# A spectral block with a feed-forward network: a weight load moved to another queue, and small work dealt out anew to three engines

## The chip, the core and the metric

The kernel runs on one core of a Trainium2 chip. TensorE (PE) multiplies matrices; VectorE (DVE), ScalarE (ACT) and GpSimd (POOL) do the element-wise work; SyncE (SP) issues most DMAs, and ScalarE and GpSimd can issue DMAs from queues of their own. Each engine runs its instructions in the order of the program and waits on semaphores for the others. The metric is the device time of one execution in microseconds; below, "the time" is the median of three runs.

## The reference, cut to what matters

One token block `x` of 2048 x 640 in bf16 goes through two halves, both modulated by a conditioning row `c`:

```
mod = silu(c) @ w_mod                     # 6 rows of 640: sa, ca, ga, sb, cb, gb
h = layernorm(x) * (1 + ca) + sa
x = x + ga * irfft2(rfft2(h) * W)         # W: 2048 x 321, complex
h = layernorm(x) * (1 + cb) + sb
x = x + gb * ((silu(h @ w_gate) * (h @ w_up)) @ w_down)    # 640 -> 1728 -> 640
```

The change touches the last four rows of `mod`: the shift `sb`, the scale `cb` and the gate `gb` of the second half (and it leaves `ga` where it was).

## The kernel before, in words

The 2048 tokens lie as 16 tiles of 128. The order of the work is written out by hand; nothing is reordered by a planner, so each engine's program is the order of the calls in the source.

**First half, to about 36 us.** Statistics and a transform over the 640 columns, then over the 128 rows of each tile; the result is `A_sb` in region `rA`.

**Spectral stage, about 36 to 63 us.** It runs over 21 groups of up to four frequencies. For each group: TensorE's `stage_a` (L567, four products, plus L580 in the last groups), VectorE's two multiplications by the filter (L592), TensorE's `stage_b` (L599), ScalarE's copy out of PSUM (`Y2`, L602), and one or two groups later TensorE's `stage_c` (L620) and a copy `evac` (mostly ScalarE, L637). GpSimd adds a constant to the transposed data before its first use (`sa_add`, L559) and makes copies of rotated values (`rot`, L648). The data of the groups 5 to 20 come from four DMA transposes on SyncE's queue (`t2_dma`, L519), one for four groups each. `stage_b` of group g and of group g + 2 use the same PSUM bank, and `stage_c` of the units (0, 1) and (2, 3) use the same two banks.

The weights of `mod` for this half and the next lie in `wm_r`, four blocks of 640 columns (gate of the first half, then shift, scale and gate of the second). Block 0 comes early. Blocks 1 and 2 (1600 KB, one DMA, L527) and block 3 (L528) stand on SyncE's queue behind the four transposes, and ahead of the tables `Htab` and `RI` (L529, L530) and the weights of the next half (L734 to L746). Blocks 1 and 2 are first read by L580 in group 17 (the fourth last), where `mod_col` computes shift and scale as columns; they end up in `modcols[:, 2]` and `one_p_cb`. Block 3 gives the gate column `modcols[:, 3]` at the end of the stage.

**Tile loop, about 63 to 82 us.** For each tile t: the inverse over rows (L669, L678) for tile t + 2, ScalarE's copy `VT` (L673), the inverse over columns (L1184, L1187), and VectorE's sum with `x` that also gives the row sums (L1189). The PSUM banks of L1184 alternate with t, so tile t + 2 needs the sum of tile t. Between them stand the preparations of the feed-forward network:

- `gdiag`: five diagonal matrices with the gate column (L1196, GpSimd, after tile 0). L1175 multiplies them by ones in tiles 5 and 7, which spreads the gate over all partitions (`gb_bc`), and `wd_fold` (L827) folds it into the down weights.
- The second layernorm of tiles 0 and 1: squares on ScalarE (L761), variance on VectorE (L765 to L767), the power -0.5 on GpSimd (L771), the normalized rows on VectorE (L775), a DMA transpose on SyncE (L789) into `h2T_first`.
- `ln2_mod(0)`: shift and scale of that first chunk, in five pieces of 128 features each. Four run on GpSimd (L797, called after tile 10), the fifth on ScalarE (L803, called after tile 13). L1001 (`gu13`, called in tile 15) is their first reader, one piece for each of its five products.
- `GS[0]`: a sum of two blocks of the gate weights, made by two DMAs from GpSimd's queue (L823), the second adding to the first; called after tiles 8 and 11. L818 reads it in the first chunk.

**Feed-forward network, 82 us to the end.** Four chunks of 2, 4, 4 and 6 tiles, the first with plain products (L1013, L891), the others with a Strassen-like scheme (L1043, L914).

Of the kernel before, what the change touches and what calls it, by code (L numbers as in the profile page):

```python
# [21 lines left out]
NC5 = 5  # L22
# [127 lines left out]
def _rev(ap, free_off, dims):  # L150
    a = ap[:]
    return bass.AP(tensor=a.tensor, offset=a.offset + free_off, ap=[list(a.ap[0])] + [list(d) for d in dims])
# [3 lines left out]
def adaln_block_kernel(ctx, tc, A_x, A_w_r, A_w_i, B_x, B_w_gate, B_w_up, B_w_down, c, w_mod, out):  # L156
    nc = tc.nc
# [26 lines left out]
    modcols = const.tile([P, 4, NC5], F32, name="modcols")  # L184
# [8 lines left out]
    identb = const.tile([P, 128], BF16, name="identb")  # L193
# [19 lines left out]
    wm_r = rM.cut(12800, [NC5, 4, D])  # L213
# [19 lines left out]
    def banks(b, n, shape=None, dt=F32):  # L233
        ap = psum[:, b:b + n, :].rearrange("p b e -> p (b e)")
        if dt == BF16:
            ap = ap.bitcast(BF16)
        if shape is not None:
            ap = ap[:, 0:int(np.prod(shape))]
            if len(shape) > 1:
                ap = ap.rearrange("p (a b) -> p a b", a=shape[0])  # L240
        return ap
# [36 lines left out]
    wm_m = wm_v[:, :, 2 * D:6 * D].rearrange("p k (i d) -> p k i d", i=4)  # L278
# [233 lines left out]
    if True:  # L512
        B2of = {}

        def t2_dma(bi):
            l0 = (1, 16, 32, 64)[bi]
            n = 15 if bi == 0 else 16
            B2b = rL.cut(4096 * bi, [16, 128]) if bi < 3 else rM.cut(6144, [16, 128])
            nc.sync.dma_start_transpose(B2b[:, :n, :], A_sb[:, l0:l0 + n, :, :, :].rearrange("p l t c r -> p l (t c r)"))  # L519
            for i in range(n):  # L520
                B2of[l0 + i] = (B2b, i, l0, n)
# [2 lines left out]
        t2_dma(1)  # L524
        t2_dma(2)
        t2_dma(3)
        nc.sync.dma_start(wm_r[:, :, 1:3, :], wm_m[:, :, 1:3, :])  # L527
        nc.sync.dma_start(wm_r[:, :, 3, :], wm_m[:, :, 3, :])  # L528
        nc.sync.dma_start(Htab[:], H_dram)  # L529
        nc.sync.dma_start(RI[:], RI_dram)  # L530
# [63 lines left out]
        def stage_b(g, PP):  # L594
            n = len(groups[g])
            yps = banks((g + 1) % 2, 1, [4, 128])
            for ps in (1, 0):
                for i in range(n):
                    nc.tensor.matmul(yps[:, i, :], lhsT=_rev(PP, 64 * n * ps + i, [[n, 128]]), rhs=identb[:],  # L599
                                     start=(ps == 1 and i == 0), stop=(ps == 0 and i == n - 1))  # L600
            Y2 = rY.cut(1024 * (g % 4), [4, 128])
            nc.scalar.copy(Y2[:, 0:n, :], yps[:, 0:n, :])  # L602
            return Y2
# [90 lines left out]
        for g in range(NG + 1):  # L694
            if g > 1:
                sa_add(g + 4)
            for W, lo, hi in {0: ((Wv, 80, 81), (Wv, 0, 16)), 1: ((Wv, 16, 32),), 3: ((Wv, 32, 48),), 11: ((Wn, 64, 80),), 13: ((Wv, 64, 80),)}.get(g, ()):
                wsum(W, lo, hi, nc.gpsimd)
                if g == 0 and hi == 81:
                    sa_add(5)  # L700
            if 0 < g < NG - 2:
                PPs[g + 2] = stage_a(g + 2)
            if g == NG - 3:
                nc.vector.tensor_copy(modcols[:, 2, :], psum[:, 2, 192:197])
                nc.vector.tensor_scalar_add(one_p_cb[:], psum[:, 4, 192:197], 1.0)
            if rots:
                l0, n, i = rots.pop(0)
                rot(l0, n, slice(0, 64), nc.gpsimd, (i,))
            if g < NG:
                Y2s[g] = stage_b(g, PPs.pop(g))  # L710
            for u, gs in enumerate(units):
                if gs[-1] + (1 if gs[0] >= NG - 2 else 3 if gs[0] == 4 else 2) == g:
                    stage_c(u)
                    evac(u)
            if g == NG - 3:
                rot(40, 8, slice(0, 64), nc.vector)
            if g == NG - 1:
                for c5 in range(NC5):
                    mod_col(psum[:, 3, 192 + c5:193 + c5], wm_r[:, :, 3], c5)
# [11 lines left out]
        gdiag = rL.cut(10496, [NC5, 128])  # L731
# [52 lines left out]
    def h2T_of(ci):  # L784
        return (h2T_next if ci else h2T_first)[:, 0:chunks[ci][1]]
# [7 lines left out]
    def ln2_mod(ci, cs=range(NC5)):  # L793
        h2T = h2T_of(ci)
        for c5 in cs:
            if ci == 0 and c5 < 4:
                nc.gpsimd.tensor_scalar(h2T[:, :, c5, :], h2T[:, :, c5, :], one_p_cb[:, c5:c5 + 1], modcols[:, 2, c5:c5 + 1],  # L797
                                        ALU.mult, ALU.add)
            elif ci and c5 % 2 == 0 or ci > 1:
                nc.vector.tensor_scalar(h2T[:, :, c5, :], h2T[:, :, c5, :], one_p_cb[:, c5:c5 + 1], modcols[:, 2, c5:c5 + 1],  # L800
                                        ALU.mult, ALU.add)
            else:
                nc.scalar.activation(h2T[:, :, c5, :], h2T[:, :, c5, :], ACT.Identity,  # L803
                                     scale=one_p_cb[:, c5:c5 + 1], bias=modcols[:, 2, c5:c5 + 1])
# [3 lines left out]
    GS = [r.cut(off, [2, GC], F16) for r, off in ((rY, 0), (rE, 25088), (rW, 42496), (rE, 31744))]  # L808
# [13 lines left out]
    def gu_dma(o, w, r, n, first):  # L822
        nc.gpsimd.dma_start(o, w[128 * r:128 * r + 128 * n, 0:GC].rearrange("(c5 dp) f -> dp c5 f", dp=P),  # L823
                            accum_op=ALU.bypass if first else ALU.add)
# [339 lines left out]
    if True:  # L1164
        s1em(2, range(0, 2))
        VTs = {0: s1er(0, 4)}
        s1em(2, range(2, 4))
        VTs[1] = s1er(1)
        for t in range(NT):
            if t and t + 2 < NT:  # L1170
                s1em(t + 2)
                if t in (5, 7):
                    g0, g1 = ((0, 3), (3, 5))[t // 7]
                    gps_ = psum[:, s1b(t + 2) + 1, 128:128 + 128 * (g1 - g0)]
                    nc.tensor.matmul(gps_, lhsT=ones[:], rhs=gdiag[:, g0:g1].rearrange("p a b -> p (a b)"), start=True, stop=True)  # L1175
                VTs[t + 2] = s1er(t + 2)
                if t in (5, 7):
                    nc.scalar.copy(gb_bc[:, 128 * g0:128 * g1], gps_)
            VT = VTs.pop(t)
            if t == NT - 1:  # L1180
                fin13 = gu13(0, at_of(0))
            ops = banks(6 * (t % 2), 2, [4, 256])[:, :, 0:160]
            for h in range(2):
                nc.tensor.matmul(ops[:, 2 * h:2 * h + 2], lhsT=VT[:, 4, :], rhs=RI[:, 1, 2 * h:2 * h + 2, :],  # L1184
                                 start=True, stop=False)
                for rr in range(2):
                    nc.tensor.matmul(ops[:, 2 * h + rr], lhsT=VT[:, 2 * h + rr, :], rhs=RI[:, 0, 2 * h + rr, :],  # L1187
                                     start=False, stop=(rr == 1))
            nc.vector.scalar_tensor_tensor(x1[:, t, :].rearrange("p (m r) -> p m r", r=4), ops.rearrange("p r m -> p m r"), 1.0,  # L1189
                                           x_sb[:, t, :].rearrange("p (m r) -> p m r", r=4), ALU.mult, ALU.add,  # L1190
                                           accum_out=st2[:, t, 0:1])
            if t == 0:
                VTs[2] = s1er(2)
                nc.gpsimd.tensor_copy(warm[:], st2[:, 0, 0:1])
                for c5 in range(NC5):
                    nc.gpsimd.tensor_scalar_mul(gdiag[:, c5], identb[:], modcols[:, 3, c5:c5 + 1])  # L1196
            if t in (8, 11):
                gu_dma(GS[0][:], B_w_gate, t // 11 * 2, 2, t == 8)
            if 1 <= t <= 2:
                ln2_sq(t - 1)  # L1200
            if t == 2:
                ln2_var(0, 2)
                ln2_pow(0, 2)
            if 3 <= t <= 4:
                ln2_xn(0, t - 3)
            if t == 4:
                ln2_tr(0)
                load_gu(512, 1024, (1,))
                load_gu(1024, 1664)
            if t in (5,7,9,11):  # L1210
                ln2_sq(2 + (5,7,9,11).index(t))
            if t in (10, 13):
                ln2_mod(0, range(4) if t == 10 else range(4, 5))
            if t == 14:
                ln2_var(2, 4)
                ln2_pow(2, 4)
            if t in (8, 9, 11, 13, 15):
                wd_fold((t - 7) // 2)
        for o, n, r, w in ((GS[2], 2, 0, B_w_gate), (UG.unsqueeze(1), 1, 4, B_w_gate), (GS[2], 2, 0, B_w_up), (UG.unsqueeze(1), 1, 4, B_w_up)):
            gu_dma(o[:], w, r, n, w is B_w_gate)  # L1220
# [101 lines left out]
```

## Time and profile before

| what | value |
|---|---|
| runs | 248.64, 248.44, 250.56 us; median 248.64 |
| profiled execution | 249.31 us; its span 247.5 us |
| granted TensorE clock | 1.0 throughout |

| stretch (us) | PE busy | DVE busy | ACT busy | POOL busy | GB/s |
|---|---|---|---|---|---|
| 0 to 36 | 34.53 | 27.69 | 23.52 | 26.57 | 332 |
| 36 to 63 (spectral stage) | 25.97 | 23.81 | 22.62 | 17.37 | 277 |
| 63 to 82 (tile loop) | 18.98 | 16.94 | 16.97 | 8.26 | 320 |
| 82 to 105 (first chunk) | 23.00 | 20.26 | 17.45 | 6.08 | 216 |
| 105 to 145 | 40.00 | 37.28 | 28.33 | 6.78 | 29 |
| 145 to 185 | 40.00 | 33.28 | 24.71 | 5.46 | 43 |
| 185 to 247.5 | 59.07 | 48.46 | 34.17 | 7.62 | 22 |

How to read it: a profile is one execution, and its times count from the start of its span. In a timeline row the first two columns are start and length in us, then engine (a "q" marks a DMA issue in that engine's queue), line, operation and operands; what stands in brackets is the idle time of the engine just before it and what ended it. The length of a DMA row is that of its issue, not of the transfer. An engine's next instruction can begin a little before the row of the one ahead ends.

### The profile page before, as it was taken

Reading aid. Unit: us, or ns where it says so; the run is one execution under the profiler, and the core shown is the slowest. Engines: PE = TensorE matmul, PEld = TensorE weight load, DVE = VectorE, ACT = ScalarE, POOL = GpSimd, SP = SyncE. Lnnn points to the kernel's source line nnn. Section 1 sums busy time; section 2 is a strip of 40 time slices with the busy share of each in tenths; the row PEclk is TensorE's granted clock in tenths of the full one; section 3 lists DMA queues with packets and bytes.
Section 4 is the critical chain, followed back from the end, with each engine's and each line's share of the span. In section 5 each row is a group of like instructions: output and inputs, shape, how many; then the busy total and the mean of one; then the engine's idle time right before and its main releaser. Section 6 shows DMA issues by size and latency. Waiting matters only on the chain.

```text
span 247.5 us, 6173 instructions
## 1 busy us (share of the span) xinstructions
PE 241.5 (98%) x2327; PEld 189.7 (77%) x2327; DVE 207.7 (84%) x516; ACT 167.8 (68%) x327; POOL 78.1 (32%) x128
## 2 busy tenths in 40 slices
PE   8999999999999999999999999999999999999994
PEld 3778877989999888688887778887765666656773
DVE  3799699988898998789989977788998787789864
ACT  3778757996989698489774488866246777773220
POOL 8577765993243605002004400000432000004400
PEclk9999999999999999999999999999999999999999
DMA  7999999999999999600005110200411000000111
GB/s 220 396 361 315 307 391 177 179 337 392 295 348 317 298 280 187 139 15 3 0 3 106 53 55 3 57 0 19 93 49 53 3 0 1 4 0 0 53 56 53
DMA packets 45760, 34.74 MB, mean 140 GB/s; under 512 B 21732, under 2 KB 42659, under 8 KB 45347
## 3 DMA queue, kind: packets, MB, share of 16 engines
q1 hardware_dynamic: 43936, 30.00, 42.7%
q0 software_dynamic: 1504, 4.28, 7.4%
q8 instruction: 18, 0.29, 0.5%
q10 hardware_dynamic: 290, 0.08, 0.1%
q14 instruction: 12, 0.09, 0.1%
HBM read 27.05 MB, written 4.72 MB: 128 GB/s over the span
## 4 chain that ended last, share of the span: by engine, by line
PE 89%; DVE 4%; DMA 3%; issue 1%; ACT 0%; POOL 0%; DVEq 0%; SPq 0%; ACTq 0%; POOLq 0%
PE psum L1043 36%; PE psum L914 19%; PE psum L1013 6%; PE psum L891 3%; DMA rM<-in_w_mod_dram 3%; PE psum L669 3%; PE psum L599 2%; PE psum L296 2%; PE psum L1184 2%; PE psum L1187 2%; PE psum L1001 2%; PE psum L567 2%; DVE rE L382 2%; PE psum L318 1%; PE psum L315 1%; PE psum L393 1%
## 5 line engine op out<-in xcount | busy, mean ns | idle before, releaser
L1043 PEld LDWEIGHTS <-rW 128*128 128x128 bf16 (+1 forms) x429 | 42.0, 98 | 12.6
L1043 PE MATMUL psum<-rW 128*128 128x256 bf16 (+1 forms) x247 | 42.2, 287 | 0.0
L940 POOL TENSOR_TENSOR rM<-rM,rL 128x320 f32<-128x320 f32 x6 | 5.4, 906 | 96.6 <-ACT rL L939 96.6
L914 PEld LDWEIGHTS <-rE 128*128 128x128 f16 (+1 forms) x196 | 19.0, 97 | 7.8
L914 PE MATMUL psum<-rE 128*128 128x320 f16 (+1 forms) x147 | 22.9, 299 | 0.0
L592 DVE TENSOR_TENSOR rM<-psum,rW 128x384 bf16<-128x384 f32 (+2 forms) x42 | 20.2, 543 | 2.7 <-PE psum L567 1.2
L1074 ACT COPY rH<-psum 128x384 f32<-128x384 f32 (+2 forms) x27 | 14.0, 517 | 7.4 <-PE psum L1043 6.0
L1081 ACT COPY rX<-psum 128x384 f32<-128x384 f32 (+2 forms) x27 | 14.0, 520 | 7.2 <-PE psum L1043 7.0
L1043 PEld LDWEIGHTS <-rE 128*128 128x128 f16 x156 | 15.3, 98 | 4.7
L1078 DVE TENSOR_TENSOR rH<-psum,rM 128x512 bf16<-128x512 f32 (+1 forms) x24 | 15.0, 624 | 4.4 <-PE psum L1043 2.2
L1097 ACT ACTIVATE rL<-psum 128x384 bf16<-128x384 f32 (+2 forms) x27 | 14.4, 533 | 5.3 <-PE psum L1043 3.4
L1082 DVE TENSOR_TENSOR rX<-psum,rX 128x384 f32<-128x384 f32 (+2 forms) x27 | 16.3, 604 | 1.6 <-ACT rX L1081 1.4
L1068 ACT COPY rM<-psum 128x384 f32<-128x384 f32 (+2 forms) x27 | 13.9, 516 | 4.2 <-PE psum L1043 4.2
L382 DVE SCALAR_TENSOR_TENSOR rE<-rE,mv,psum 128x648 bf16<-128x648 f32 (+1 forms) x17 | 14.2, 840 | 2.1 <-PE psum L318 1.7
L1043 PE MATMUL psum<-rW,rE 128*128 128x256 bf16 (+1 forms) x78 | 15.6, 290 | 0.0
L1043 PE MATMUL psum<-rE,rY 128*128 128x256 f16 (+1 forms) x78 | 15.6, 290 | 0.0
L338 ACT COPY rE<-psum 128x640 bf16<-128x640 bf16 x16 | 11.1, 693 | 6.1 <-PE psum L336 5.1
L1098 ACT ACTIVATE rL<-rX 128x384 bf16<-128x384 f32 (+2 forms) x27 | 15.1, 559 | 0.0
L1013 PE MATMUL psum<-rW 128*128 128x256 bf16 x130 | 14.5, 272 | 0.0
L602 ACT CAST rY<-psum 128x512 bf16<-128x512 f32 (+2 forms) x21 | 11.8, 574 | 3.9 <-PE psum L599 3.6
L1189 DVE SCALAR_TENSOR_TENSOR rM<-psum,rX 128x640 f32<-128x640 f32 x16 | 13.0, 820 | 1.7 <-PE psum L1187 1.6
L883 DVE TENSOR_TENSOR rA<-psum,rM 128x320 bf16<-128x320 f32 (+1 forms) x27 | 12.1, 472 | 2.4 <-PE psum L891 2.3
(223 smaller groups left out, 666.5 us busy)
## 6 DMA issues: line engine op xcount, KB each, us to landing
out_dram<-rA SPq DMA_DIRECT2D x31, 80.0 KB, 1.6
rM<-in_w_mod_dram SPq DMA_DIRECT2D x3, 800.0 KB, 10.2
rX<-in_A_x_dram SPq DMA_DIRECT2D x3, 640.0 KB, 7.4
rA<-in_B_w_down_dram SPq DMA_DIRECT2D x2, 960.0 KB, 14.4
rY<-in_B_w_gate_dram POOLq DMA_DIRECT2D x2, 832.0 KB, 7.9
rM<-in_w_mod_dram SPq DMA_DIRECT2D x1, 1600.0 KB, 7.3
rW<-in_B_w_gate_dram SPq DMA_DIRECT2D x2, 640.0 KB, 7.1
rW<-in_B_w_up_dram SPq DMA_DIRECT2D x2, 640.0 KB, 7.1
```

Of the source, the lines that this page charges most:

```text
L382: nc.vector.scalar_tensor_tensor(Zv[:, h], Cv[:, h], mv[:, t, 0:1], zps[:, h], ALU.mult, ALU.subtract)
L592: nc.vector.tensor_tensor(PP[:, :, hl], xv[:, :, hl], in1, ALU.mult)
L914: nc.tensor.matmul(o, lhsT=lhs[rows(k), k], rhs=rhs[rows(k), k], start=start and k == ks[0], stop=stop and k == ks[-1], skip_group_check=True)
L1013: nc.tensor.matmul(gu[u], lhsT=Wgu[:, u, c5, ff * 128:(ff + 1) * 128], rhs=h2T[:, :, c5, :], start=(c5 == 0), stop=(c5 == NC5 - 1))
L1043: nc.tensor.matmul(o[:, f], lhsT=w, rhs=b, start=(start and f == 0 and i == 0), stop=(stop and f == len(groups[g]) - 1 and i == len(ops) - ...
L1068: nc.scalar.copy(c0, X)
L1074: nc.scalar.copy(c2, X)
L1078: nc.vector.tensor_tensor(c11, Z, c0, ALU.add)
L1081: nc.scalar.copy(c3, X)
L1082: nc.vector.tensor_tensor(c22, Y, c3, ALU.add)
L1097: nc.scalar.activation(g21, X, ACT.Silu, scale=-1.0)
L1098: nc.scalar.activation(g22, c22, ACT.Silu, scale=-1.0)
```

## The change

Four edits:

1. The DMA of blocks 1 and 2 of `wm_r` leaves SyncE's queue and is issued from ScalarE's queue, right behind the `Y2` copy of group 2 of the spectral stage. It waits for no transfer that is still on its way at that point.
2. Of the five pieces of `ln2_mod(0)`, the pieces 0 and 1 stay on GpSimd, piece 2 goes to VectorE (the line L800 of before), pieces 3 and 4 are on ScalarE. The first four are called after tile 12 (before: 10), the fifth after tile 13 as before. In ScalarE's program piece 3 stands between the `VT` copies of tiles 14 and 15, piece 4 behind the latter; in VectorE's, piece 2 stands between the sums of tiles 12 and 13.
3. The five diagonals go from GpSimd to VectorE: two behind the sum of tile 0, three behind that of tile 1.
4. The first DMA of `GS[0]` is called after tile 0 (before: 8), the second after tile 12 (before: 11), there behind the pieces.

No other instruction changes its place in any engine's program.

```diff
@@ spectral stage, SyncE's queue
         t2_dma(3)
-        nc.sync.dma_start(wm_r[:, :, 1:3, :], wm_m[:, :, 1:3, :])
         nc.sync.dma_start(wm_r[:, :, 3, :], wm_m[:, :, 3, :])
@@ loop over the groups
                 Y2s[g] = stage_b(g, PPs.pop(g))
+                if g == 2:
+                    nc.scalar.dma_start(wm_r[:, :, 1:3, :], wm_m[:, :, 1:3, :])
@@ ln2_mod
-            if ci == 0 and c5 < 4:
+            if ci == 0 and c5 < 2:
                 nc.gpsimd.tensor_scalar(...)
-            elif ci and c5 % 2 == 0 or ci > 1:
+            elif ci == 0 and c5 == 2 or ci and c5 % 2 == 0 or ci > 1:
                 nc.vector.tensor_scalar(...)
             else:
                 nc.scalar.activation(...)
@@ tile loop
                 nc.gpsimd.tensor_copy(warm[:], st2[:, 0, 0:1])
-                for c5 in range(NC5):
-                    nc.gpsimd.tensor_scalar_mul(gdiag[:, c5], identb[:], modcols[:, 3, c5:c5 + 1])
-            if t in (8, 11):
-                gu_dma(GS[0][:], B_w_gate, t // 11 * 2, 2, t == 8)
+                gu_dma(GS[0][:], B_w_gate, 0, 2, True)
+            if t < 2:
+                for c5 in range(2 * t, 2 + 3 * t):
+                    nc.vector.tensor_scalar_mul(gdiag[:, c5], identb[:], modcols[:, 3, c5:c5 + 1])
@@ tile loop, later
-            if t in (10, 13):
-                ln2_mod(0, range(4) if t == 10 else range(4, 5))
+            if t in (12, 13):
+                ln2_mod(0, range(4) if t == 12 else range(4, 5))
+            if t == 12:
+                gu_dma(GS[0][:], B_w_gate, 2, 2, False)
```

## The prediction

> **What bounds it now.** The page's first part has TensorE busy 98% of the span, so time is lost only where TensorE stands still or is given more to do. I read the chain that ended last, in order of time, from 47 us on:
>
> ```profile
> 47.29 0.59 ACT rY L602
> 48.06 7.32 DMA rM<-in_w_mod_dram
> 55.43 0.40 PE psum L580 x10
> ```
>
> Columns: start, length, what. From 55.43 the chain stays on TensorE up to 244 us; this is the last place where a transfer holds it. The 7.32 us is the load's whole length; what it costs is in the list of waits (total, times, longest), two rows for one wait:
>
> ```profile
> PEld L580 <- DMA rM<-in_w_mod_dram: 0.8, 1, 0.8
> PE psum L580 <- DMA rM<-in_w_mod_dram: 0.6, 1, 0.6
> ```
>
> TensorE's timeline gives the start of L567's first product of that group, 54.59; elsewhere L580 follows 0.08 later (56.38, 56.46), so it would have begun at 54.67 and began at 55.43: 0.76 lost. The SyncE queue shows why the load is late:
>
> ```profile
> 37.10 7.00 SPq L519 DMA_TRANSPOSE rL<-rA  x3
> 44.21 3.81 SPq L519 DMA_TRANSPOSE rM<-rA  x1
> 48.06 0.59 SPq L527 DMA_DIRECT2D rM<-in_w_mod_dram  x1
> 48.70 0.52 SPq L528 DMA_DIRECT2D rM<-in_w_mod_dram  x1
> ```
>
> It stands behind four transposes whose issue fills the queue from 37.10 to 48.02. ScalarE's timeline shows the place where the change puts it:
>
> ```profile
> 41.63 1.22 ACT L602 CAST rY<-psum 128x512 bf16<-128x512 f32 x2 [0.37 <-PE psum L599]
> 43.46 0.59 ACT L602 CAST rY<-psum 128x512 bf16<-128x512 f32 x1 [0.61 <-PE psum L599]
> 43.97 1.01 ACT L637 CAST rE<-psum 128x1024 bf16<-128x1024 f32 x1
> ```
>
> The load is issued behind the second copy of the first row (group 2), ahead of the third (group 3). ScalarE stood idle there for 0.61.
>
> **Load, on ScalarE.** Issue: 0.59 on SyncE, 0.34 for ScalarE's own store at 244.70; I take 0.59. It fits the 0.61 of idle time: nothing added, if the issue isn't held (rivals). The load starts about 42.9, 5.2 earlier, and lands about 50.2 by its old 7.32. It is needed at 54.67. Its cover is 4.4 us deep.
>
> Removed: 0.76 of TensorE's wait. VectorE must follow: its product of that group began at 56.19 after 1.12 idle, so it was free at 55.07; it can move by the whole 0.76 (to 55.43) and is still 0.36 idle. I take 0.75. Ahead of 55 us nothing is saved.
>
> **Load, off SyncE.** All behind it is issued 0.64 earlier (48.70 to 48.06), and 1.6 MB less stand ahead. That matters: with TensorE 0.75 earlier, Htab (issued 49.26, 12.2 to land: 61.5) is wanted at 62.3 and RI (49.83, 12.4: 62.2) at 62.6. Both hold even unmoved; L528's load (58.9) is wanted at 61.4. Price zero.
>
> **Gate diagonals, from GpSimd to VectorE.** GpSimd loses 2.95 (five at 0.60). VectorE gains five of 128 columns. Lower bound 0.11 each, the pitch of L648's pair (two of 128 in 0.30, 0.19 long); upper bound 0.26, L439's length (162 columns, also scaled by a column). L419's four, scaled by a column too, take 0.75, 0.16 apart; I take 0.15. Two go behind tile 0's L1189 (66.30 to 66.60; the next starts 66.84: free). Three go behind tile 1's (67.59 to 68.04), where tile 2's L1189 started at 67.88: 0.16 late. Queued behind them are L765 to L767, the power on GpSimd, L775 and tile 4's L1189, for which TensorE has almost no room:
>
> ```profile
> 70.00 0.08 DVE L1189 DVE_READ_ACCUMULATOR rM<-psum,rX 128x1 f32 x1
> 70.28 0.61 DVE L775 TENSOR_SCALAR rL<-rM,st,rstd 128x640 bf16<-128x640 f32 x1 [0.20 <-POOL rstd L771]
> 70.81 0.82 DVE L1189 SCALAR_TENSOR_TENSOR rM<-psum,rX 128x640 f32<-128x640 f32 x1
> ```
>
> Tile 4's sum ends at 71.63, and TensorE's L1184 of tile 6, in the same bank, starts at 71.72. But the power L771 ran at 69.53 only because the diagonals held GpSimd until 69.56; its input was there at 69.34. With them gone it starts at 69.34 plus 0.16: no later than before. So zero at 0.15; at 0.26 each, 0.48 late at tile 2, 0.3 at tile 4, about 0.25 on TensorE.
>
> **First gate sum (L823).** Issued about 66.7 instead of 70.20 (0.84 of GpSimd, which then waits for the power anyway), and its second half after two pieces instead of four. The first reader is L818 at 90.17; the second half, issued 80.66 and landing in about 8, has 1.5 to spare already. Zero.
>
> **The five pieces.** Before:
>
> ```profile
> 78.22 2.50 POOL L797 TENSOR_SCALAR rW<-rW,one_p_cb,modcols 128x256 bf16<-128x256 bf16 x4 [7.17 <-DMA rW<-rL]
> 80.44 0.60 ACT L803 ACTIVATE rW<-rW,modcols,one_p_cb 128x256 bf16<-128x256 bf16 x1
> ```
>
> GpSimd ended at 80.72; TensorE's L1001 started at 80.79 although its last L1187 (80.57) let go at 80.63: 0.16 lost. In the same clock after: GpSimd's two end at 79.64; VectorE's one, 0.3 to 0.54 (L800, twice the columns, is 0.54), goes between L1189s at 80.02 and ends by 80.6, wanted at 80.85. ScalarE becomes last: L803 at 79.53, the copy L673 of tile 15 at 80.03 (80.72 at its end, wanted at 81.2), L803 again 80.62 to 81.22. L1001's fifth product, formerly at about 81.22, starts at 81.27. So +0.05; the 0.16 changes hands. The transpose that feeds the pieces (landed 78.2) must also move: its inputs, L775, move with TensorE, so by 0.75.
>
> **Sum.** -0.75 + 0.05 = -0.70. This execution took 249.31 (span 247.5, 1.8 around it): 248.6. It lies 0.67 over the median of the three, 248.64, so **247.9**.
>
> **Rival 1: the issue is held until SyncE's third transpose is issued.** The issue times of transposes (7.00 for three) keep the pace of their data, so something behind the queue paces them, and ScalarE's issue may need the same thing. Then it ends at 44.10 + 0.59 = 44.69 and L602 of group 3 starts 1.23 late. L637 behind it frees the banks for L620 (45.04) 1.2 late, and L567 of group 8 and the products wait: VectorE, which ran 21 products without a gap from 39.12, loses about 1.2. It gets back its own 0.19 idle at 48.93 and the 1.12 at 55.07, 1.31 in all: net -0.1, **248.6**. Against: at the start ScalarE's L244 (0.72 to 1.25) and SyncE's L246 (0.73 to 1.13) were issued side by side. [...]
>
> **Rival 2: held through the fourth transpose; slower.** SyncE's gap between the two is 0.1; if it comes first again, ScalarE's issue ends at 48.02 + 0.59 = 48.6 and group 3's copy is 5.15 late: 5.15 - 1.31 = +3.8, **252.5**. From an issue end of 43.46 + 1.31 = 44.77 the change loses, by one us for each; past 47.3 it is slower by over 1%.
>
> **Rival 3: the load takes the transposes' turns.** The stage's windows:
>
> ```profile
> 43.00:44.00 1.00, 1.00 (x20) 1.00 (x18) 1.00 (x3) 0.54 (x2) 1.00 (x2) 1.00 1.13 215
> 45.00:46.00 1.00, 1.00 (x17) 0.96 (x16) 1.00 (x3) 0.96 (x3) 0.98 (x4) 1.00 0.07 8
> 52.00:53.00 1.00, 1.00 (x20) 1.00 (x18) 1.00 (x3) 0.99 (x3) 1.00 (x3) 1.00 1.04 404
> ```
>
> The last columns are DMA share and GB/s: transposes fill the engines (1.13) at 215 GB/s; the load alone gets 404, so 1.6 MB is 4.1 us. If all of it comes first, the third transpose (landed at latest 41.6 + 5.8 = 47.4) lands at 51.5; the products that need it start at 50.59: 0.9, with GpSimd's add up to 1.4 late. The fourth (49.4) lands at 53.5, its add ran at 53.16. That is -0.7 + 0.5 to 1.4: **248.4 to 249.3**. Against: the empty second at 45, and that in turns neither gets all. [...]
>
> **Chances.** Forecast 0.50, rival 1 0.26, rival 3 0.10, rival 2 0.09, others 0.05. A change under 1% (2.5 us) can hardly be told from none: the three runs span 248.44 to 250.56. Faster by over 1% needs more than all of TensorE's waits here: 0.02. Slower: rival 2 and some of the others, 0.12. Same: 0.86. Low end: both waits gone (0.92) and 0.5 for the scatter of runs, 247.2. High end: rival 3's 249.3 and the same scatter, 249.8; rival 2 is left out. The forecast's own range is 247.4 to 248.4.
>
> **What would show it.** L580 starts 0.08 behind its group's first L567, and L567 of group 8 starts near 45.5 (rivals 1 and 2: 46.7 or 50). ScalarE's issue row: 0.6 long, or 1.8, or 5. POOL L559 waits for a DMA at 49 or 53: rival 3. L1184 of tile 6 directly behind L678: the diagonals are free. L1001 waits for L803, not L797. I would be wrong altogether if L602 of group 3 moves by over 1.3 us, or if TensorE's stall at 55.4 comes back later in the same size.

## The result, and the profile after

The changed kernel takes 251.37 us (median of 16 runs, 250.31 to 254.07); the kernel before, on the same chip, 249.68 (16 runs, 248.44 to 251.19). The ratio is 1.008, with a 95% interval of 1.0057 to 1.0103: slower by 1.7 us by the medians (2.0 by the ratio), where 0.7 less was forecast. Medians are of all runs, while ratios and their intervals leave out runs over 1.5% above the fastest of their kernel (so `split_sp` below has 250.87 and a ratio of 1.0003); the six longest of the changed kernel's 16 runs (251.91 to 254.07), all with a granted clock of 0.993, are in both. The profiled executions are 250.91 (span 249.1) and 249.31 (span 247.5), 1.6 apart, so the pair of traces is a fair picture of the medians.

In the changed kernel the lines up to the new issue (L711) are one lower than before (L558 is the add of before's L559, L566 its L567, L579 its L580, L601 its L602), those behind it one higher (L790, L798, L804, L1002, L1185, L1188, L1190); the diagonals are L1199.

TensorE's starts at the same instructions show where the time went:

| TensorE starts | before | after | difference |
|---|---|---|---|
| `stage_a` of group 13, the first on the third transpose | 50.59 | 52.91 | +2.32 |
| first product of `mod_col` with shift and scale | 55.43 | 57.01 | +1.58 |
| first product of tile 6 in the tile loop | 71.72 | 73.29 | +1.57 |
| first product of the first chunk (`gu13`) | 80.79 | 82.56 | +1.77 |
| first down product of that chunk | 96.21 | 97.84 | +1.63 |
| last product | 243.35 | 244.98 | +1.63 |

Of the 2.32, 0.36 is there before the load is issued at 42.63 (TensorE's first product of group 3 starts at 41.02 instead of 40.66) and owes nothing to it; at group 5 the other kernels of this study lie 0.06 ahead of before to 0.93 behind it, so this much differs between executions. 1.96 is new. Then 0.75 comes back, 0.2 goes at the first chunk, and 0.14 comes back inside it, which I did not follow further.

The chain that ended last, in order of time (start, length, what), over the place where the loss is:

```profile
39.75 1.95 SPq L519
41.70 0.04 issue
41.74 10.77 DMA rL<-rA
52.52 0.08 issue
52.59 0.28 POOL rL L558
52.87 0.05 issue
52.91 0.50 PE psum L566 x4
```

The load is off the chain. In its place stands the third transpose, 10.77 us long, then GpSimd's add, then group 13. In the list of waits (total, times, longest) it is TensorE's largest, and the wait for the load is not in the list any more:

```profile
PE psum L566 <- POOL rL L558: 1.8, 1, 1.8
```

GpSimd's timeline says what the add itself waited for (in brackets: idle time, and what ended it):

```profile
52.59 0.27 POOL L558 TENSOR_TENSOR rL<-rL,SA 128x16 bf16<-128x16 bf16 x1 [2.52 <-DMA rL<-rA]
```

Before, that add had no wait:

```profile
49.17 0.62 POOL L559 TENSOR_TENSOR rL<-rL,SA 128x16 bf16<-128x16 bf16 x1
```

The SyncE queue of the kernel after, start and length of the issues:

```profile
37.02 7.20 SPq L519 DMA_TRANSPOSE rL<-rA  x3
44.34 7.97 SPq L519 DMA_TRANSPOSE rM<-rA  x1
52.35 0.59 SPq L527 DMA_DIRECT2D rM<-in_w_mod_dram  x1
52.98 0.51 SPq L528 DMA_DIRECT2D rH<-tab_H  x1
```

The first three transposes are issued as before; the fourth takes 7.97 instead of 3.81, over the time (44.34 to 52.31) in which its queue moves far fewer packets than before (138 from 48 to 49 us, see below). ScalarE's timeline where the load is issued:

```profile
41.99 1.22 ACT L601 CAST rY<-psum 128x512 bf16<-128x512 f32 x2 [0.64 <-PE psum L598]
42.63 0.42 ACTq L711 DMA_DIRECT2D rM<-in_w_mod_dram  x1
43.82 0.58 ACT L601 CAST rY<-psum 128x512 bf16<-128x512 f32 x1 [0.61 <-PE psum L598]
```

The issue takes 0.42, in the middle of SyncE's row of three transposes (37.02 to 44.22), and the next copy waits the same 0.61 for TensorE as before. So ScalarE loses nothing; the loss is on the DMA engines. The list of DMA issues on the page ends each row with the us from issue to landing:

```profile
rM<-in_w_mod_dram ACTq DMA_DIRECT2D x1, 1600.0 KB, 9.4
```

It landed at 42.63 + 9.4 = 52.0, 2.7 ahead of the 54.67 at which before would have wanted it. What it did on the way is read from the packets that each queue moved in one microsecond. First the kernel after from 48 to 49 us (queue, packets, MB, share of 16 engines; q10 is ScalarE's queue, q1 SyncE's), in the answer on DMA queues:

```profile
q10 hardware_dynamic: 141, 0.36, 91.4%
q1 hardware_dynamic: 138, 0.04, 15.5%
```

The same view of the kernel before, from 47 to 48, when the transposes are alone:

```profile
q1 hardware_dynamic: 1132, 0.29, 127.4%
```

In that microsecond one packet of the load went for one packet of a transpose (141 and 138). By MB and packets the first has 2560 bytes (0.36 MB / 141; the two blocks of a row), the second 256 (0.29 MB / 1132). The transposes fall from 1132 packets per us to 138, an eighth, until the load's packets run out at about 51 us (in its last full microsecond, 50 to 51, it is 131 of the load to 244). Here the clock is not part of it: the stage's windows of the kernel after (TensorE, its weight loads, VectorE, ScalarE and GpSimd busy, the granted clock, DMA share, GB/s) have 1.00 throughout:

```profile
45.00:46.00 1.00, 1.00 (x17) 0.88 (x15) 1.00 (x4) 1.00 (x3) 0.75 (x2) 1.00 1.02 312
...
48.00:49.00 1.00, 0.88 (x16) 0.76 (x15) 1.00 (x3) 0.97 (x3) 0.76 (x3) 1.00 1.07 396
52.00:53.00 1.00, 0.09 (x1) 0.09 (x2) 0.00 (x0) 0.26 (x1) 0.41 (x2) 1.00 1.28 280
```

At 48 the DMA engines move twice the bytes of before (396 GB/s against 199), and TensorE has still work from the second transpose; at 52 it stands still, with the engines at 1.28 on the transposes that were pushed back.

The wait for the load is gone. TensorE's timeline where `mod_col` is first called:

```profile
56.92 0.25 PE L566 MATMUL psum<-Ktab,rM 128*128 128x192 bf16 x1
57.01 0.39 PE L579 MATMUL psum<-sc_col,rM 128*128 128x1 bf16 x10
```

It follows 0.09 behind its group's first product. The diagonals, on VectorE's timeline:

```profile
67.87 0.41 DVE L1199 TENSOR_SCALAR rL<-identb,modcols 128x128 bf16<-128x128 bf16 x2
...
69.16 0.57 DVE L1199 TENSOR_SCALAR rL<-identb,modcols 128x128 bf16<-128x128 bf16 x3
```

Their pitch is (0.57 - 0.41) = 0.16 us. TensorE's difference to before is +1.58 ahead of them and +1.57 at tile 6: they cost nothing. Last, ScalarE's timeline at the end of the tile loop, and TensorE's:

```profile
81.11 0.61 ACT L804 ACTIVATE rW<-rW,modcols,one_p_cb 128x256 bf16<-128x256 bf16 x1
81.62 0.69 ACT L672 CAST rL<-psum 128x640 bf16<-128x640 f32 x1
82.19 0.61 ACT L804 ACTIVATE rW<-rW,modcols,one_p_cb 128x256 bf16<-128x256 bf16 x1
```

```profile
82.16 0.30 PE L1188 MATMUL psum<-rH,rL 128*128 128x160 bf16 x2
82.56 0.71 PE L1002 MATMUL psum<-rW,Wp 128*128 128x256 bf16 x5
```

The chunk's first product starts 0.40 behind the row of the last product of tile 14 (0.22 before: 80.57 and 80.79), and 0.25 behind the end of ScalarE's copy of tile 15 (82.31). Before it stood 0.25 behind that copy too (80.54 to 80.79), on ScalarE and TensorE:

```profile
79.85 0.69 ACT L673 CAST rL<-psum 128x640 bf16<-128x640 f32 x1 [0.21 <-PE psum L678]
```

```profile
80.79 0.71 PE L1001 MATMUL psum<-rW,Wp 128*128 128x256 bf16 x5
```

Its PSUM bank, 2, is one that the copy reads.

### The profile page after: what moved, and what is told of

Read it like the earlier page. It is cut to its first block, busy times and chain, and to the rows that moved or that the text cites. A ratio compares the mean times of both kernels' runs of the same rounds, so it can differ in the third digit from the quotient of the medians.

```text
span 249.1 us, 6171 instructions
## 1 busy us (share of the span) xinstructions
PE 241.5 (97%) x2327; PEld 189.4 (76%) x2327; DVE 208.8 (84%) x522; ACT 168.3 (68%) x328; POOL 73.8 (30%) x121
## 4 chain that ended last, share of the span: by engine, by line
PE 86%; DMA 6%; DVE 4%; SPq 1%; issue 1%; ACT 1%; POOL 0%; DVEq 0%
PE psum L1044 36%; PE psum L915 19%; PE psum L1014 6%; DMA rL<-rA 4%; PE psum L892 3%; PE psum L668 3%; DMA rM<-in_w_mod_dram 2%; PE psum L1185 2%; PE psum L1002 2%; PE psum L598 2%; PE psum L1188 2%; PE psum L566 1%; PE psum L393 1%; DVE rE L382 1%; PE psum L318 1%; PE psum L394 1%
## 5 line engine op out<-in xcount | busy, mean ns | idle before, releaser
L601 ACT CAST rY<-psum 128x512 bf16<-128x512 f32 (+2 forms) x21 | 11.8, 573 | 5.5 <-PE psum L598 5.2
L1190 DVE SCALAR_TENSOR_TENSOR rM<-psum,rX 128x640 f32<-128x640 f32 x16 | 13.0, 820 | 0.9 <-PE psum L1188 0.7
```

## The experiments

The theory after the result: the load's packets take turns, one for one, with those of the third and fourth transposes, and a packet of the load is ten times as long. The rivals were that something else of the change costs the time, that any load on ScalarE's queue at this place does it, whatever its size, and that the order inside one queue matters rather than the second queue. A second question is the 0.2 at the first chunk. Each run stands beside runs of the kernel before on the same chip; ratios are to those.

**The first edit alone, and the others alone.** `load_only` is the kernel before with edit 1, `rest_only` the kernel after with the load back on SyncE's queue:

```diff
 load_only: before
-        nc.sync.dma_start(wm_r[:, :, 1:3, :], wm_m[:, :, 1:3, :])
...
                 Y2s[g] = stage_b(g, PPs.pop(g))
+                if g == 2:
+                    nc.scalar.dma_start(wm_r[:, :, 1:3, :], wm_m[:, :, 1:3, :])
 rest_only: after, with these lines the other way round
```

> The kernel before with the load of blocks 1 and 2 issued from ScalarE's queue behind group 2, nothing else. Theory (the load takes the transposes' turns: on each DMA engine the two queues go one packet by one, 2560 bytes against 256): the whole loss is here. GpSimd's add L558 waits for the third transpose until about 52.5, TensorE stands still for about 1.8 us at group 13, the wait at L580 (0.76) is gone: +1.2 us, ratio about 1.005. Rival (the loss comes from edits 2 to 4): no wait at L558 and the kernel is 0.7 us faster, ratio 0.997.

> Edits 2 to 4 without edit 1: the load stays on SyncE's queue. Theory: no wait at L558, the 0.76 at L580 stays; the piece put between the copies of tiles 14 and 15 makes the copy of tile 15 about 0.2 late, and L1002 with it, so +0.2 us, ratio 1.000 to 1.002. Rival (the loss comes from these edits): +1.2 to +2 us, ratio 1.005 to 1.008.

`load_only`: 251.48 us, ratio 1.0087 (1.0053 to 1.0122). `rest_only`: 250.37, ratio 1.0024 (0.9997 to 1.0051). TensorE's waits in `load_only` have the same entry as the kernel after:

```profile
PE psum L566 <- POOL rL L558: 1.8, 1, 1.8
```

and none for the load. In `rest_only` that entry is missing, and another is there:

```profile
PE psum L1001 <- POOL rW L797: 0.7, 1, 0.7
```

So the loss is the first edit's: `load_only` has all of it, and the interval of `rest_only` includes 1. In `rest_only` the load stands where it stood, landed at 47.78 + 7.4 = 55.2 (before 55.4), and cost only 0.16, not 0.75: L580 began at 55.23, its group's first product at 54.99, since this execution came to group 17 later by 0.40. The wait that the change removes is thus the shorter, the later TensorE comes to group 17. The other wait is new: GpSimd's pieces came late, because the transpose that feeds them (L789) landed 8.0 us after its issue (72.01 to 80.0), instead of 6.0 before and 5.0 in the kernel after (here and below landing is counted to about the start of GpSimd's first piece, 0.1 to 0.2 more than the list of issues has). I come back to it.

**Packets of half the length.** `two_loads` is the kernel after with the load as two DMAs, so that each packet is one block's row of 1280 bytes; bytes, queue and place are the same:

```diff
                 if g == 2:
-                    nc.scalar.dma_start(wm_r[:, :, 1:3, :], wm_m[:, :, 1:3, :])
+                    nc.scalar.dma_start(wm_r[:, :, 2, :], wm_m[:, :, 2, :])
+                    nc.scalar.dma_start(wm_r[:, :, 1, :], wm_m[:, :, 1, :])
```

> The changed kernel with its load cut into two DMAs of one block each, so that a row is 1280 bytes instead of 2560; the same bytes, in the same place on ScalarE's queue (about 0.4 us more of issue). Theory (packet by packet): while both queues are busy they move about 230 packets per us each instead of 141; the transposes get about twice as many turns, the third lands about 1.3 us earlier and L558 starts near 51.2 instead of 52.6; TensorE's stall at group 13 falls from 1.8 to about 0.5. Rival (only the bytes ahead count, or the two kinds of transfer exclude each other): L558 still starts at 52.4 to 52.8.

251.51 us, ratio 1.0062 (1.0035 to 1.009). The queues from 46 to 47 us, in the view used above:

```profile
q10 hardware_dynamic: 238, 0.30, 82.4%
q1 hardware_dynamic: 238, 0.06, 26.8%
```

Again one for one, at 238 turns per us instead of 141; so the transposes keep 238 packets per us instead of 138. GpSimd's add for the third transpose ran at 51.79 (52.59 after, its wait 1.39 instead of 2.52), and TensorE's stall is 0.7 instead of 1.8: the direction and nearly the size that turns by packet give (51.2 and 0.5 expected). So 1.1 us of the stall went with the length of a packet, the bytes being the same (one trace on each side). The ratios' intervals overlap, so the gain in time is read from the traces and not proved by the medians.

**Half the load.** `half_act` is the kernel before with block 2 alone on ScalarE's queue; block 1 stays on SyncE's, behind the transposes:

```diff
-        nc.sync.dma_start(wm_r[:, :, 1:3, :], wm_m[:, :, 1:3, :])
+        nc.sync.dma_start(wm_r[:, :, 1, :], wm_m[:, :, 1, :])
...
+                if g == 2:
+                    nc.scalar.dma_start(wm_r[:, :, 2, :], wm_m[:, :, 2, :])
```

> The kernel before, in which only block 2 (shift or scale, half the load, 640 packets of 1280 bytes) goes to ScalarE's queue behind the copy of group 2; block 1 stays where the load stood on SyncE's queue. Theory (the two queues take turns packet for packet, so what the transposes lose is as many turns as the load has packets, times the length of one of the load's packets): half the packets, each half as long, cost the transposes about 640 x 16 engines' share = 2 us or less instead of 4.4; the third transposes land at about 50.5 at the latest, GpSimd waits less than 0.6 for them and TensorE not at all or under 0.3; the wait for the load is gone too (its second half lands near 52.5 behind the transposes); span about 0.5 to 0.75 shorter than before's 247.5 as far as 55.4 us. Rival (what costs is that any load stands in another queue at that place, whatever its size): TensorE still stalls about 1.8 us at group 13.

250.73 us, ratio 1.0049 (1.0024 to 1.0074). GpSimd's timeline, and TensorE's at the first call of `mod_col`:

```profile
50.72 0.26 POOL L559 TENSOR_TENSOR rL<-rL,SA 128x16 bf16<-128x16 bf16 x1 [1.08 <-DMA rL<-rA]
```

```profile
55.13 0.39 PE L580 MATMUL psum<-sc_col,rM 128*128 128x1 bf16 x10
```

The third transpose was late by less than with the whole load (GpSimd waited 1.08, against 2.52 and the expected 0.6 at most), TensorE stood idle for 0.34 ahead of that group (the trace puts that down to a product on VectorE; the add for the transpose ended at 50.98, just ahead of the group's start at 51.04), and the load's wait is gone: at 55 us this kernel is 0.3 ahead of before. Size counts, then; a load as such doesn't. What it gained it lost at the first chunk, where TensorE waited 1.5 for GpSimd's four pieces: L789's transpose landed 8.4 after its issue.

**The same place in SyncE's own queue.** `same_queue` is the kernel before with the load between the second and the third transpose:

```diff
         t2_dma(1)
+        nc.sync.dma_start(wm_r[:, :, 1:3, :], wm_m[:, :, 1:3, :])
         t2_dma(2)
         t2_dma(3)
-        nc.sync.dma_start(wm_r[:, :, 1:3, :], wm_m[:, :, 1:3, :])
```

> The kernel before with the load on SyncE's queue but ahead of the third of the four transposes, issued about 41.7, so that it has the same start as in the kernel after without a second queue. Theory: in one queue it goes first and alone at about 0.4 MB per us, 4.1 us, and the third transposes land behind it at 50.5 to 51.5, the fourth at 52.5 to 53.5: TensorE stalls 0.5 to 1.3 at group 13 (1.8 in the kernel after, where the turns slow the transposes for 6 us), the wait for the load is gone; span 0 to 0.6 over before's. Rival (the order does not matter, only that the load is among the transposes): 1.8 as in after. Second rival (inside one queue the load overlaps with the transposes without cost): no stall, 0.75 gained.

251.47 us, ratio 1.006 (1.0036 to 1.0083). The same kernel was run a second time:

> The kernel of same_queue once more, for a profile at full clock. Its ratio of 1.006 is 1.5 us over before, more than the 0 to 0.6 that the theory gave. Theory, mended: the third transposes lie wholly behind the load and the last of the second's packets, so that they land near 51.5 to 52.5 and TensorE stalls 1.3 to 1.8 at group 13; the load's own packets stand in SyncE's queue alone, at some 150 per us, with no transpose packet between them. Rival (a late transpose of the feed-forward network makes the rest of the 1.5): the stall at group 13 is under 1 and TensorE waits over 0.7 for GpSimd's pieces at the first chunk.

250.89 us, ratio 1.0046 (1.0011 to 1.0082). Here the queue from 45 to 46 us holds the load alone, in its place in the line:

```profile
q1 hardware_dynamic: 156, 0.40, 101.8%
```

and GpSimd's add, then TensorE's group 13:

```profile
52.31 0.26 POOL L559 TENSOR_TENSOR rL<-rL,SA 128x16 bf16<-128x16 bf16 x1 [2.13 <-DMA rL<-rA]
```

```profile
52.63 0.50 PE L567 MATMUL psum<-Ktab,rL 128*128 128x192 bf16 x4 [1.35 <-POOL rL L559]
```

The first expectation was too small (0.5 to 1.3 of stall and 0 to 0.6 of time, against 1.35 and 1.5 us by the ratio of the first run); the second holds. The load ahead of the transposes in one queue cost TensorE 1.35 at group 13, beside them in another 1.8: in both it is 1.6 MB between group 13 and its data. And this run gives the load's rate alone, 156 packets per us. With the transposes' 1132 alone, one packet of each takes 1/156 + 1/1132 us = 7.3 ns, counted over all DMA engines together, that is 137 turns per us; the kernel after has 138 to 142 in its undisturbed microseconds. For packets of 1280 bytes at the same 0.40 MB per us, 1/312 + 1/1132 gives 245; `two_loads` has 238 to 250 in its three fullest microseconds, `half_act` up to 228 (beside 312 of the transposes, just before its load ran out). So in these microseconds the turns came about as fast as the two packets' times alone give. That leaves out the microseconds in which both nearly stop (46 to 48 in the kernel after).

**The change, four groups later.** `late_change` is the kernel after with the issue behind the copy of group 6, when most packets of the transposes have gone:

```diff
-                if g == 2:
+                if g == 6:
                     nc.scalar.dma_start(wm_r[:, :, 1:3, :], wm_m[:, :, 1:3, :])
```

> The kernel after, with the load issued from ScalarE's queue behind the copy of group 6 instead of group 2, about 48 us, when most of the transposes' packets have gone (in before the last went by at 49.4). Theory (the loss is the packets that the transposes still have in hand times the turn of 120 ns): only the rest of the fourth transpose (some 600 packets) shares turns with the load, it lands 2 to 3.5 us later than in before, at 51.5 to 53, and its add on GpSimd is first wanted at 53.2: no stall at group 13; the load, 4.1 us alone and not much slowed, lands by 53.5, ahead of its want at 54.7: the wait of 0.75 is gone as well; L579 starts near 54.7 plus what the start of the stage brings; the rest as the kernel after; the time 1.6 to 2.0 under after's, about before's less 0.3 to 0.5, if the feed-forward network's transpose lands early. Rival (any load from ScalarE's queue in this stage costs 1.8 to 2): the stall is there at group 13 or 17, and the time stays at after's.

249.53 us, ratio 0.9979 (0.9961 to 0.9998): the only kernel of this study that is under the kernel before by its interval, by 0.2%, and 1.8 under the kernel after by the medians. With an interval that ends at 0.9998, one of eleven, the gain over before is no more than likely; that the loss is gone is clear. ScalarE's timeline and TensorE's:

```profile
47.13 0.39 ACTq L711 DMA_DIRECT2D rM<-in_w_mod_dram  x1
```

```profile
55.18 0.25 PE L566 MATMUL psum<-Ktab,rM 128*128 128x192 bf16 x1
55.26 0.39 PE L579 MATMUL psum<-sc_col,rM 128*128 128x1 bf16 x10
```

The third transpose's add ran at 49.76 without a wait, the fourth's at 53.74 without a wait although that transpose landed 2.7 us later than before (7.8 from issue to landing, at 52.1): it had the room. The load's wait is gone. The queue is the change's; the moment alone differs. The traces have the same span, 247.5: this execution was 0.59 behind before at group 5, 0.17 ahead at `mod_col`, and level again at the chunk (80.81 and 80.79).

The expectation had some 600 packets of the transposes share turns with the load, at 120 ns a turn, an estimate: 16 engines by the 141 to 138 turns per us of the kernel after are 113 to 116 ns. In fact the load's first packets went at 49.0, when the transposes' data was all but through (41 packets left). Ahead of the fourth transpose's landing at 52.1 SyncE's queue moved 32 packets of under 512 bytes each from 51 to 52 us, by my reading the transpose's last (the load, too, has 16 packets beyond its 640 rows). Ahead of them that queue moved nothing for about two microseconds; the view from 50 to 51 us has the load alone:

```profile
q10 hardware_dynamic: 147, 0.38, 97.1%
```

Why the last packets came so late isn't known.

**The first chunk, and the transpose that feeds it.** `split_sp` is the kernel before with the load cut in two on SyncE's queue, at its old place; `four_pool` is that with the 640 KB load of gate weights (L749) moved from ahead of L789's transpose to behind it; `combo` is `four_pool` with edits 2 to 4; `combo_bank` is `combo` with the first chunk's banks counted from 4:

```diff
 split_sp: before
-        nc.sync.dma_start(wm_r[:, :, 1:3, :], wm_m[:, :, 1:3, :])
+        nc.sync.dma_start(wm_r[:, :, 2, :], wm_m[:, :, 2, :])
+        nc.sync.dma_start(wm_r[:, :, 1, :], wm_m[:, :, 1, :])
 four_pool: split_sp
-    load_gu(512, 1024, (0,))
...
                 ln2_tr(0)
-                load_gu(512, 1024, (1,))
+                load_gu(512, 1024)
 combo_bank: combo
-    ring = [2]
+    ring = [4]
```

> The kernel before with its load cut in two on SyncE's own queue, behind the transposes as before: block 2 (read in group 17) first, then block 1 (read in group 18). Theory: the transposes are undisturbed; block 2 lands near 53, before L580 wants it at 54.7, and block 1 near 55.5, wanted at about 55.7. The wait of 0.76 goes and nothing comes in its place: 0.7 us faster, ratio about 0.997. Rival (the wait at L580 is worth nothing, something else sets the end): the same time as before.

> The kernel before with the load cut in two on SyncE's queue (as in split_sp) and, new, the 640 KB load of gate weights that stands ahead of the feed-forward network's first transpose moved behind it. Theory (that transpose lands late when the queue's backlog and GpSimd's gate sums are ahead of it; 640 KB at about 0.36 MB per us are 1.8 us): it lands within 5 to 7 us of its issue, at 78.5 at the latest, instead of 9.2 us in split_sp; GpSimd's four pieces end by 81, TensorE loses 0.2 to 0.4 at the first chunk instead of 2.0; the time is 0.75 under before's, ratio 0.997. Rival (the landing is delayed by something else, the backlog has no part): it lands at 80 to 81 as in split_sp, and TensorE waits 1.5 to 2 for the pieces; ratio 1.000 to 1.004.

> As four_pool, and with edits 2 to 4 of the change (pieces shared among three engines, diagonals on VectorE, gate sums called elsewhere). Theory: the transpose lands at 78.5 or before; the pieces are done in time; TensorE's first product of the chunk starts 0.34 behind the last product of tile 14 as in the kernel after (0.16 before), because ScalarE's piece stands ahead of its copy for tile 15; the time is 0.5 to 0.75 under before's, ratio 0.997, and 0 to 0.2 above four_pool's where the transpose lands early in both. Rival (sharing the pieces is worth something by itself even with an early transpose): combo is faster than four_pool by 0.2 or more.

> As combo, with the first chunk's banks counted from 4 instead of 2, so that its first product does not use the bank that ScalarE's copy for tile 15 reads. Theory (that product waits for the copy): it starts directly behind the last product of tile 14, 0.2 to 0.3 earlier than in combo; the rest of the chunk follows by the same, unless tile 15's sums, which use banks 6 and 7, hold the third and fourth products. Rival (it waits for ScalarE's or VectorE's piece, or for the transposed data): the gap stays 0.3.

`split_sp`: 250.87 us, ratio 1.0003 (0.9973 to 1.0033). The wait for the load is gone without any other queue (the first piece to land is the one that is read first). The time isn't less, against the 0.7 us expected. In its profiled execution (251.26 us) L789's transpose landed 9.2 us after its issue, and the four pieces on GpSimd came out one by one behind it, each waited for; whether that holds in the other runs, from 249.00 to 253.13, isn't shown. TensorE's waits:

```profile
PE psum L1002 <- POOL rW L798: 2.0, 4, 1.2
```

`four_pool`: 249.77, ratio 0.9999 (0.997 to 1.0027); its profiled execution 248.87, span 247.1. The transpose landed at 77.71, 6.1 from its issue, and no wait for pieces is left. `combo`: 250.18, ratio 1.0022 (0.9986 to 1.0058); profiled 248.72, span 247.0, landing 6.5 after the issue. By their profiled executions both are 0.4 to 0.6 under before's; by their medians neither is, and the runs of `combo` scatter from 248.62 to 252.58. So a gain from taking the load's wait away in this manner isn't shown; that the wait was as small as 0.16 in one execution would fit. Nor is it shown that the backlog has a part: with the gate load moved the transpose took 5.6 to 6.5 us in three traces, without it 5.0 to 9.2 in nine. The two ranges overlap, and what sets the landing stays open.

The chunk's own 0.2 is settled. From tile 6's first product to the first product of the chunk TensorE takes:

| kernels without a wait for pieces | us |
|---|---|
| before, `same_queue2`, `four_pool` (pieces as before) | 9.07, 9.06, 9.06 |
| `load_only` (pieces as before, and late) | 9.20 |
| after, `two_loads`, `late_change`, `combo` (pieces shared) | 9.27, 9.28, 9.27, 9.27 |
| `combo_bank` (pieces shared, other bank) | 9.01 |

In `load_only` the copy isn't the cause: its product stands 0.38 behind the copy's end, since tile 14 began 0.25 late, for VectorE's sum of tile 12 behind a fold that took 0.70 beside GpSimd's pieces. In `combo` the chunk's product follows the row of tile 14's last by 0.21 only, against 0.40 in the kernel after (0.34 in the expectation, which counts from the row's second product), but tile 14 itself began 0.18 late, for VectorE's sum of tile 12; the product still stands 0.25 behind the copy's end (80.02 and 80.27), and so the sum is the same 9.27. In `combo_bank` the chunk starts as soon as the copy ends; ScalarE's timeline, then TensorE's:

```profile
80.22 0.69 ACT L674 CAST rL<-psum 128x640 bf16<-128x640 f32 x1
```

```profile
80.76 0.30 PE L1187 MATMUL psum<-rH,rL 128*128 128x160 bf16 x2
80.90 0.83 PE L1001 MATMUL psum<-rW,Wp 128*128 128x256 bf16 x5
```

The copy ends at 80.91 and the product begins at 80.90; in the copy's bank it began 0.25 behind the copy's end in the kernels before and after and in `combo`, and here the 0.25 is gone. So it is the copy, put back by the piece ahead of it on ScalarE, and not a piece, that the product waited for. The other bank is no gain all the same: `combo_bank` takes 251.04, ratio 1.005 (1.0021 to 1.008). Its waits show one price that was foreseen as a condition, the bank of tile 15's sum, and one that wasn't, the gate and up weights loaded later:

```profile
PE psum L1013 <- DVE rM L1189: 1.0, 1, 1.0
PE psum L1013 <- DMA rW<-in_B_w_up_dram: 0.7, 1, 0.7
```

## Why the prediction was wrong, step by step

**The load, on ScalarE: the step that failed.** The text took the load's cover, "4.4 us deep", for the price of the move: it asked when the load lands and is wanted, and found it early. It was early (52.0 against 54.67). What the move costs to those already on the DMA engines stood only in rival 3. The sum there was -0.70; the measured balance is +1.6 in the profiled executions, of which 1.96 is the late third transpose. `load_only` (1.0087) and `late_change` (0.9979) show that it is this edit, and this moment of it.

**Rival 3** had the mechanism and got 0.10. It is the one that came true, and it was under-priced too: 1.96 where its sum has 0.5 to 1.4 (the 0.5 has no working), since the third transpose landed at 52.5, not at "51.5 at most". Two things were missing. Its bound let the load pass at 404 GB/s while the transposes stand; in fact both crawl in turns, and the load's packets pass from 44.5 to 51.6 us, 7 us instead of 4.1. And both queues nearly stopped from 46 to 48 (47 and 68 packets of the load per us, against 141), much as SyncE's queue did before from 45 to 46 (30 packets). What speaks "against", that in turns neither gets all, was the error in the weighing: the turns were by packet, and the side with 256-byte packets kept an eighth of its pace, 138 of 1132 per us. The sizes of both packets could have been had from the trace of before, as MB by packets (0.29 by 1132 from 47 to 48, 0.40 by 158 from 52 to 53). The place in a queue decided more here than when the load was issued: it also decided whose packets went first, for 1.8 us of TensorE.

**Removed wait, 0.75.** Right for the execution that it was read from: L579 stands 0.09 behind its group, and the difference to before falls from 2.32 to 1.58, by 0.74. VectorE followed, as argued. Taken as a constant it was too much: it is 0.16 in the execution of `rest_only`.

**Rivals 1 and 2, the issue held.** Wrong, and the forecast right against them: 0.42 for the issue, no copy moved. No trace shows ScalarE's issue held by SyncE's transposes: with them in the course of being issued the load took 0.42 in `load_only` too and 0.39 in `late_change`, and two loads in a row took 0.41 and 0.57 (`two_loads`).

**Load, off SyncE: price zero.** Right by another road. The rest of SyncE's queue was not issued 0.64 earlier but 3.7 later (Htab at 52.98 instead of 49.26), because the fourth transpose's issue held it for 7.97. The tables landed in time all the same: Htab at 52.98 + 8.4 = 61.4, before at 61.5, since it took less time behind its issue (8.4 against 12.2).

**Diagonals and first gate sum, zero.** Right; pitch 0.16 (0.15 taken).

**The five pieces, +0.05.** Mis-sized: +0.20, in every kernel that has them. The text said "the 0.16 changes hands" and let the copy of tile 15 move behind a piece, asking only whether tile 15's products want it (81.2). The bank that the copy reads is the one into which the chunk's first product writes; that wait was the 0.16, and it grew. What speaks for the edit wasn't in the text: where L789's transpose lands late, two pieces on GpSimd cost TensorE 0.7 (`rest_only`) and four cost 1.5 to 2.0 (`half_act`, `split_sp`).

**The base.** The sum was laid on the median of three runs, 248.64; over 16 runs the kernel before has 249.68. About 1.0 of the distance between 247.9 and 251.37 is that, and 2.4 is the change itself: -0.7 forecast against +1.7.

## What to carry to other kernels

Before a load is started earlier, count the packets of whatever is then in flight and the bytes of one packet on each side: here 256-byte packets went one for one with packets of 2560 bytes (138 and 141 per us), and a load that landed 2.7 us before it was wanted still cost TensorE a stall of 1.8 at the work ahead of it. Ask of a moved load not only what waits for it but what it passes; here, four groups later on the same queue, the load's wait was gone and the stall did not come. And where an instruction is put ahead of a copy out of PSUM, look who next writes that bank, not only who reads the copy; here that was 0.2 us.

## What the runs showed of the hardware

- Two queues with work shared the DMA engines packet for packet: 141 to 138 per us with packets of 2560 and 256 bytes, 238 to 238 with 1280 and 256. Shortly before a load ran out it was 131 to 244 (after, 50 to 51 us) and 228 to 312 (`half_act`, 48 to 49). This is measured on data packets only: in `late_change` 32 small packets of SyncE's queue came about two microseconds behind the transposes' data, while the load moved 147 packets per us. The turns came near what the two packets' times alone give: 138 to 142 per us against 137 by 156 and 1132 alone, and 238 to 250 against 245, which is an estimate with 312 for packets of 1280 bytes at the same 0.40 MB per us.
- A DMA of 1.6 MB was issued on ScalarE in 0.42 us while SyncE was issuing transposes.
- With transposes issued and not yet landed, the queues all but stopped for about one to two microseconds between 45 and 49 us in the traces of before, after and five others (30 packets from 45 to 46 before; 15 and 13 from 47 to 48 in `load_only`). The runs don't say why.
- The same transpose (L789) took 5.0 to 9.2 us from issue to landing, with much the same work around it; with 9.2 TensorE waited 2.0 us in all for the four pieces on GpSimd (`split_sp`), and this spread may be part of why single runs of one kernel lie two to four us apart. This wasn't tested.
- Some of VectorE's instructions were longer while GpSimd ran its pieces: the same fold of 640 columns took 0.68 us beside them and 0.48 after them (`combo`), the piece of 256 columns 0.58 beside them (`late_change`) and 0.34 without (the kernel after), though 0.55 also in `combo`, where it began 0.24 behind the end of GpSimd's row. The sum out of PSUM (L1189) was not: 0.81 beside the pieces in `combo` and 0.81 after them.
